# Query tiles, score products and the next batch's probabilities moved in a fused attention and mixer kernel

## The chip, the cores and the metric

One core of a Trainium2 chip runs the whole program. The metric is the time of one execution on the device in microseconds (us); the time of a kernel is the median of its runs.

## What is computed

There are eight batches (B = 8) of 576 tokens with 8 heads of 64 channels and 32 memory slots. Each batch goes through an attention with a small memory, a low-rank token mixer with a two-layer network of width 2048, and a gated network with a spatial product:

```python
a = exp(phi - max(phi, axis=tokens)); a = a / (sum(a, axis=tokens) + 1e-9)
k_m, v_m = a^T k, a^T v                       # per head, 32 x 64
scores = q k_m^T / 8; attn = softmax(scores)  # 576 x 32 per head
x = concat_heads(attn v_m)                    # 576 x 512
u = x + (x^T U V)^T
y = u + relu(u w_ch1) w_ch2                   # 512 -> 2048 -> 512
h = relu(y w_in); u2, v = halves of h
vn = (v - mean) / sqrt(var + 1e-6)
out = (u2 * (w_spatial vn + b_spatial)) w_out
```

## The kernel before

Most products are made in float16 with each operand split into a high and a low part, three products for one. TensorE (PE) is given work nearly without a gap, batch after batch. For batch b the stages are: the first-weight product with relu (in batches 2 to 7 line 954, its results taken out by lines 958 to 966), the second-weight product (line 920 in batches 2 to 7, in a form with seven block products; line 875 in batch 1; line 815 in batch 0), both in two halves of 288 tokens; then the input product of the gate (lines 1107 and 1178), the spatial product (line 1219) and the output product (line 1249).

The attention of the next batch is the generator `att(b + 1)`. It is not a stage of its own: while batch b is worked on, the code of batch b calls `step(nxt)` after every few products, and each call runs `att` up to its next `yield`. So a `yield` more or less, or a call of `step` more or less, moves the attention's instructions against the products of batch b. A scheduler of the framework then sets the order of each engine from this order and the dependences; inside an engine the order is fixed, and an instruction whose input is late holds all that stands behind it.

In `att`, in this order: the maximum over tokens and the exponentials of phi; the products with keys and values (line 578); a transpose (line 598) and its copies `kT` and `vmt32` (lines 604 and 607); the score products `scores(i)` (line 622) for three groups of token tiles, G = (0, 1), (2, 3), (4,), each into two PSUM tiles of the pool `at`, which has three; ScalarE (ACT) copies them to `sT` (line 627); PE transposes `sT` back (line 648); VectorE (DVE) takes the row maximum (652), subtracts it (655), ACT makes the exponential (657), DVE the row sum, its reciprocal and the normalised probability (663 to 667), ACT the high half `ahl[.., 0, :]` (671) and DVE the low half (672). Then PE mixes all five tiles with U (line 681, ten matmuls into one PSUM tile), ACT and DVE make `pst` from it (686, 687), and the generator gives "Z" and then "W". After "W" the mixed probabilities `apr` are made in three pieces (PE lines 538 and 544, maxima on DVE, then 721 and 722) and `att_vmu` (line 740). `step` without `w=True` does not go past "W"; before the change all calls of `step` with `w=True` are in the gate's input product, which the list `V_ORDER` orders.

The query tiles come from DRAM on SyncE's (SP) queue. `load_q(b, s)` takes one of two buffers of the tag "q": tiles 0 and 1 are loaded ahead, and `scores` asks for tile s + 2 when tile s is used, so that the loads of tiles 2 and 3 can only start when the products with tiles 0 and 1 have been made. From batch 3 on, tile 4 has a place of its own in the large buffer `gw`, columns 8064 to 8319, and is loaded in `pre(b)` (line 1472), a batch ahead.

In batch 1 the kernel also prepares, beside its last second-weight product, the block sums of the second weight (`s_prep`, lines 1035 to 1058): four times a load of 1 MB from DRAM (`w2d`), sums and splits on DVE and ACT, and a store. The function `both` calls `step(nxt)` and one step of `s_prep` 32 times in that product.

Of the kernel before, what the change touches and what calls it, by code (L numbers as in the profile page):

```python
# [30 lines left out]
def mixer_kernel(  # L31
# [216 lines left out]
    AT = {}  # L248
# [300 lines left out]
    def att(b):  # L549
# [64 lines left out]
        def scores(i):  # L614
            r = rows(G[i][0])
            n = r * len(G[i])
            ps = [at_tile() for e_ in range(2)]
            for k, s in enumerate(G[i]):
                for p in range(4):
                    for e_ in range(2):  # L620
                        r0 = slice(64 * e_, 64 * e_ + 64)
                        pe.matmul(ps[e_][32 * p:32 * p + 32, k * r:(k + 1) * r], kT[r0, 32 * p:32 * p + 32],
                                  a["q"][s][r0, p, :r], start=True, stop=True)
                load_q(b, s + 2)
            sT[i] = tmp()
            for e_ in range(2):
                act.activation(sT[i][:, e_ * 256:e_ * 256 + n], ps[e_][:, 0:n], func=ACTF.Copy)
# [14 lines left out]
        for gi, grp in enumerate(G):  # L642
# [15 lines left out]
            yield  # L658
            if gi < 2:
                scores(gi + 1)  # L660
            yield
# [9 lines left out]
            act.activation(ahl[:r, s0:s0 + n, 0, :], exs, func=ACTF.Copy)  # L671
            dve.tensor_tensor(out=ahl[:r, s0:s0 + n, 1, :], in0=exs, in1=ahl[:r, s0:s0 + n, 0, :], op=ALU.subtract)
            yield
            yield
        yield
# [3 lines left out]
        for s in range(NST):  # L679
# [3 lines left out]
            if s == 2:  # L683
                yield
        pst = tp.tile([128, 256], F16, tag="pst", name="pst")
        act.activation(pst, pps[:, 0:256], func=ACTF.Copy, scale=2.0 ** -22)
        dve.scalar_tensor_tensor(out=pst[64:96], in0=pps[64:96, 0:256], scalar=2.0 ** -22, in1=pst[64:96],
                                 op0=ALU.mult, op1=ALU.subtract)
        yield
        yield  # L690
# [777 lines left out]
    def pre(b):  # L1468
        if b < B:
            if b > 2:  # L1470
                t = AT[b]["q"][4] = gw[:, 8064:8320].rearrange("p (g c) -> p g c", g=4)
                sp.dma_start(t, qT[b, :, :, 512:S])
            gen[b] = att(b)
            next(gen[b])
# [20 lines left out]
    def step(g, w=False):  # L1495
        if w or not hold.get(id(g)):
            if next(g, None) == "W":
                hold[id(g)] = True
# [74 lines left out]
    for b in range(B):  # L1573
# [3 lines left out]
        elif b == 1:  # L1577
            sq = s_prep()
            w1_phase(b, 0, nofill)

            def both():
                step(nxt)
                next(sq, None)
# [156 lines left out]
```

## Time and profile before

| | |
|---|---|
| median of 3 runs | 1147.14 us (1144.29 to 1148.76) |
| profiled execution | 1148.05 us, span of its records 1146.1 us |
| PE busy, share of the span | 97% |
| DVE, ACT, POOL busy | 74%, 54%, 8% |
| mean granted clock of TensorE | 0.997 |

The span is the time from the first to the last recorded instruction; the profiled execution's own time is 1.95 us longer. Engines work beside each other, so their shares do not add up; with PE at 97%, what matters is each of its gaps and what ended it.

### The profile page before, as it was taken

What the parts mean: (1) busy time and instruction counts of PE and PEld (TensorE: products, weight loads), DVE (VectorE), ACT (ScalarE), POOL (GpSimd) and SP (SyncE); (2) the same over time, 40 slices, a digit from 0 to 9 for tenths busy, and PEclk for the clock granted to TensorE, in tenths of its full rate; (3) what the DMA queues carried; (4) which work ended last, traced back from release to release, by engine and by line L of the source; (5) the groups of instructions that cost most, each with busy time, mean ns of one, the idle gap of its engine ahead of it and who ended that gap; (6) DMA issues with size and microseconds to landing.
All of it is one profiled execution on the core that took longest, in us unless ns stands there. A gap on an engine that the chain in (4) does not pass through costs nothing.

```text
span 1146.1 us, 29691 instructions
## 1 busy us (share of the span) xinstructions
PE 1114.4 (97%) x12365; PEld 867.6 (76%) x12365; DVE 844.5 (74%) x2217; ACT 620.0 (54%) x1350; POOL 89.5 (8%) x316
## 2 busy tenths in 40 slices
PE   8899999999999999999999999999999999999998
PEld 6466667767667896788867887678967888679966
DVE  5767688869786786867776787867868677766854
ACT  4768764736456454564465453564545643653543
POOL 2101011000010001100010000100011000100000
PEclk9999999999999999999999999999999999999999
DMA  9769741340526331442315303253204303130201
GB/s 357 309 258 343 264 170 58 117 146 28 193 76 205 93 112 36 146 150 79 126 59 194 122 22 129 93 203 98 113 35 141 138 20 127 38 116 2 102 27 42
DMA packets 54854, 145.72 MB, mean 127 GB/s; under 512 B 7808, under 2 KB 37248, under 8 KB 43584
## 3 DMA queue, kind: packets, MB, share of 16 engines
q1 hardware_dynamic: 54208, 143.16, 35.4%
q8 instruction: 96, 1.57, 0.6%
q10 hardware_dynamic: 512, 0.67, 0.2%
q14 instruction: 38, 0.31, 0.1%
HBM read 120.32 MB, written 23.49 MB: 125 GB/s over the span
## 4 chain that ended last, share of the span: by engine, by line
PE 74%; DVE 11%; ACT 6%; DMA 5%; issue 2%; POOL 1%; SPq 0%; ACTq 0%; DVEq 0%; POOLq 0%
PE mm L920 17%; PE mm L954 13%; PE mm L1219 10%; PE mm L1249 8%; PE mm L1178 6%; PE mm L1107 5%; PE mm L815 3%; DMA qt<-in_qT_dram 2%; PE at L756 2%; PE at L578 2%; PE mm L792 1%; PE mm L875 1%; DMA q<-in_qT_dram 1%; PE mm L838 1%; DVE yhl L1074 1%
## 5 line engine op out<-in xcount | busy, mean ns | idle before, releaser
L920 PE MATMUL mm<-gw,w2r 128*128 128x144 f16 x2304 | 170.6, 226 | 0.0
L920 PEld LDWEIGHTS <-w2r 128*128 128x128 f16 x2304 | 152.6, 98 | 7.9 <-issue 2.7
L954 PE MATMUL mm<-apr,z 128*128 128x288 f16 x1152 | 155.1, 286 | 0.0
L954 PEld LDWEIGHTS <-z 128*128 128x128 f16 x1152 | 109.7, 98 | 28.3 <-issue 2.0
L958 ACT ACTIVATE wsr<-mm 128x288 f32<-128x288 f32 x192 | 78.3, 408 | 95.2 <-PE mm L954 51.4
L920 PE MATMUL mm<-gw,wa 128*128 128x144 f16 x1728 | 128.8, 226 | 0.0
L1219 PE MATMUL mm<-wsr,gw 128*128 128x288 f16 x896 | 114.3, 286 | 1.7 <-ACT gw L1182 1.6
L920 PEld LDWEIGHTS <-wa 128*128 128x128 f16 x1728 | 111.1, 98 | 4.6 <-issue 2.0
L1219 PEld LDWEIGHTS <-gw 128*128 128x128 f16 x896 | 85.6, 98 | 32.1 <-issue 9.6
L1178 PE MATMUL mm<-yhl,gw 128*128 128x288 f16 x768 | 99.4, 286 | 0.0
L1249 PE MATMUL mm<-ghl,wa 128*128 128x288 f16 x768 | 97.8, 286 | 0.0
L1249 PEld LDWEIGHTS <-wa 128*128 128x128 f16 x768 | 74.4, 98 | 22.8 <-issue 3.8
L1178 PEld LDWEIGHTS <-gw 128*128 128x128 f16 x768 | 73.4, 98 | 18.6 <-issue 0.6
L960 DVE TENSOR_TENSOR wsr<-wsr 128x288 f32<-128x288 f32 x96 | 44.0, 459 | 57.7 <-ACT wsr L958 57.7
L1107 PE MATMUL mm<-gw,yhl 128*128 128x512 f16 x384 | 85.6, 379 | 0.0
L942 DVE TENSOR_TENSOR gw<-wsr,gw 128x720 f16<-128x720 f32 x96 | 85.5, 901 | 0.0
L1234 ACT ACTIVATE ghl<-gw,ysc 128x288 f16<-128x288 f32 x64 | 34.2, 535 | 83.2 <-DVE gw L1233 83.2
L941 ACT ACTIVATE gw<-wsr 128x720 f16<-128x720 f32 x96 | 76.4, 795 | 0.5
L1107 PEld LDWEIGHTS <-yhl 128*128 128x128 f16 x384 | 36.9, 98 | 41.8 <-DVE yhl L1074 0.5
L815 PE MATMUL mm<-gw,w2r 128*128 128x288 f32 x256 | 66.7, 409 | 0.0
L1113 DVE BATCH_NORM_STATS2 tiny<-tmp 128x6 f32<-128x512 f32 (+1 forms) x40 | 25.6, 639 | 46.5 <-ACT tmp L1111 46.4
L815 PEld LDWEIGHTS mm<-gw,w2r 128*128 128x128 f32 x256 | 47.3, 190 | 15.2 <-issue 2.1
(312 smaller groups left out, 1857.3 us busy)
## 6 DMA issues: line engine op xcount, KB each, us to landing
wa<-w1d SPq DMA_DIRECT2D x22, 1024.0 KB, 5.1
kvt<-in_kv_dram SPq DMA_DIRECT2D x28, 516.0 KB, 5.3
gw<-wid SPq DMA_DIRECT2D x12, 1024.0 KB, 7.9
wsr<-wsd SPq DMA_DIRECT2D x7, 1440.0 KB, 6.4
out_dram<-tmp SPq DMA_DIRECT2D x64, 144.0 KB, 1.9
qt<-in_qT_dram SPq DMA_DIRECT2D x28, 256.0 KB, 3.5
gw<-in_w_dram SPq DMA_DIRECT2D x6, 1024.0 KB, 8.3
wa<-wod SPq DMA_DIRECT2D x6, 1024.0 KB, 4.7
```

Of the source, the lines that this page charges most:

```text
L815: pe.matmul(ps, w2r[:, f, d * 128:(d + 1) * 128], AT[0]["g"][:, f, :], start=False, stop=(f == 15))
L920: pe.matmul(ps[:, dd * QH:(dd + 1) * QH], w(c, dd, 1 - x), gs[:, m, c, y, :], start=(first and c == 0 and dd == 0 and i == 0), stop=(end a ...
L941: act.activation(h, X[:, 3:8], func=ACTF.Copy)
L942: dve.tensor_tensor(out=gs[:, 2:7, c, 1, :], in0=X[:, 3:8], in1=h, op=ALU.subtract)
L954: pe.matmul(ps, a["z"][:, k, x, f * 128:(f + 1) * 128], a["apr"][:, k, y, sl], start=(i == 0), stop=(i == 5))
L958: act.activation(o, pair(ps), func=ACTF.Relu, scale=CG)
L960: dve.tensor_tensor(out=X[:, 4:6], in0=X[:, 2:4], in1=X[:, 1:3], op=ALU.subtract)
L1107: pe.matmul(ps, yhl[:, k, x, s * 128:(s + 1) * 128], wih[:, k, 0, 1 - y, :], start=(i == 0), stop=(i == 11))
L1178: pe.matmul(ps, wih[:, k, 1, 1 - x, d * 128:(d + 1) * 128], a["yhl"][:, k, y, sl], start=(i == 0), stop=(i == 11))
L1219: pe.matmul(pss[d], vn[:, s, x if s < 4 else 0, ds], wsh[:, s, th, 1 - y, :], start=(s == 0 and i == 0), stop=(s == 4 and i == 1))
L1234: act.activation(ghl[:, d, 0, sl], u2, func=ACTF.Identity, scale=sgt)
L1249: pe.matmul(ps, (wo0 if b else woh)[:, k, 1 - x, d * 128:(d + 1) * 128], a["ghl"][:, k, y, sl], start=(i == 0), stop=(i == 11))
```

## The change

Five edits. From batch 3 on the third query tile (tile 2) gets a place of its own in `gw`, columns 8320 to 8831, and is loaded in `pre(b)` beside tile 4. When tile 0 is used, tile 3 is asked for; when tile 1 is used, tile 2 (which from batch 3 on is already there). The score products of the later groups are issued after the low and high halves of the first group: from batch 3 on both groups at once, in batches 1 and 2 one group after each group's halves. In the mix with U a second `yield` stands after the third tile, and one `yield` fewer behind `pst`. In batch 1 `both` steps the attention of batch 2 in its calls 1 to 7 and then in every third, from call 9 on with `w=True`.

```diff
@@ -621,7 +621,7 @@
                         r0 = slice(64 * e_, 64 * e_ + 64)
                         pe.matmul(ps[e_][32 * p:32 * p + 32, k * r:(k + 1) * r], kT[r0, 32 * p:32 * p + 32],
                                   a["q"][s][r0, p, :r], start=True, stop=True)
-                load_q(b, s + 2)
+                load_q(b, 3 - s if s < 2 else s + 2)
             sT[i] = tmp()
             for e_ in range(2):
                 act.activation(sT[i][:, e_ * 256:e_ * 256 + n], ps[e_][:, 0:n], func=ACTF.Copy)
@@ -656,8 +656,6 @@
                               in1=mxs[:r, :n * 8].unsqueeze(2).to_broadcast([r, n * 8, M]), op=ALU.subtract)
             act.activation(ex[:r, 0:n * 256], ex[:r, 0:n * 256], func=ACTF.Exp, scale=0.125)
             yield
-            if gi < 2:
-                scores(gi + 1)
             yield
             sm = tiny(16)
             dve.tensor_reduce(out=sm[:r, :n * 8], in_=ex3, axis=AX.X, op=ALU.add)
@@ -670,7 +668,12 @@
             s0 = grp[0]
             act.activation(ahl[:r, s0:s0 + n, 0, :], exs, func=ACTF.Copy)
             dve.tensor_tensor(out=ahl[:r, s0:s0 + n, 1, :], in0=exs, in1=ahl[:r, s0:s0 + n, 0, :], op=ALU.subtract)
+            if gi == 0 and b > 2:
+                scores(1)
+                scores(2)
             yield
+            if gi < 2 and b < 3:
+                scores(gi + 1)
             yield
         yield
         yield
@@ -682,11 +685,11 @@
                           start=(s == 0 and y == 0), stop=(s == NST - 1 and y == 1))
             if s == 2:
                 yield
+                yield
         pst = tp.tile([128, 256], F16, tag="pst", name="pst")
         act.activation(pst, pps[:, 0:256], func=ACTF.Copy, scale=2.0 ** -22)
         dve.scalar_tensor_tensor(out=pst[64:96], in0=pps[64:96, 0:256], scalar=2.0 ** -22, in1=pst[64:96],
                                  op0=ALU.mult, op1=ALU.subtract)
-        yield
         yield
         yield "Z"
 
@@ -1468,8 +1471,9 @@
     def pre(b):
         if b < B:
             if b > 2:
-                t = AT[b]["q"][4] = gw[:, 8064:8320].rearrange("p (g c) -> p g c", g=4)
-                sp.dma_start(t, qT[b, :, :, 512:S])
+                for s, o in ((2, 8320), (4, 8064)):
+                    t = AT[b]["q"][s] = gw[:, o:o + 4 * rows(s)].rearrange("p (g c) -> p g c", g=4)
+                    sp.dma_start(t, qT[b, :, :, s * 128:s * 128 + rows(s)])
             gen[b] = att(b)
             next(gen[b])
 
@@ -1578,8 +1582,12 @@
             sq = s_prep()
             w1_phase(b, 0, nofill)
 
+            nb = [0]
+
             def both():
-                step(nxt)
+                nb[0] += 1
+                if nb[0] < 8 or nb[0] % 3 == 0:
+                    step(nxt, nb[0] > 8)
                 next(sq, None)
 
             y0 = w2_phase(b, 0, lambda: step(nxt), lambda f: fl.until(s2, min(f + 3, 16)))
```

The calls of `att` are numbered by the batch they prepare: `b > 2` in `att` is what runs during batches 2 to 6.

**ACT's queue, first half of the second-weight product of batch 2 (the same in batches 3 to 6).** Names are as in the section on the kernel; 128x256 is a group of two tiles, 128x64 the group of one. Before:

```order
L999 ACTIVATE y_4430<-mm 128x2x144
L604 ACTIVATE t1k<-at 64x128 x2
L627 ACTIVATE tmp<-at 128x256 x2
L637 ACTIVATE vmt<-t1k,sc 128x128
L657 ACTIVATE tmp<-tmp 128x512
L627 ACTIVATE tmp<-at 128x256 x2
L671 ACTIVATE ahl<-tmp 128x2x256
L958 ACTIVATE wsr<-mm 128x288
```

And now:

```order
L1002 ACTIVATE y_4431<-mm 128x2x144
L604 ACTIVATE t1k<-at 64x128 x2
L627 ACTIVATE tmp<-at 128x256 x2
L637 ACTIVATE vmt<-t1k,sc 128x128
L657 ACTIVATE tmp<-tmp 128x512
L627 ACTIVATE tmp<-at 128x256 x2
L627 ACTIVATE tmp<-at 128x64 x2
L669 ACTIVATE ahl<-tmp 128x2x256
```

The copies of the third group (128x64) have come forward from the second half to the place right behind those of the second group. On PE at this place the order was four transposes (line 648), 12 products of line 920, the 16 score products of group 1, and products again; now it is four transposes, 24 products, the 16 score products of group 1, the first 4 of group 2, 4 products, the last 4 of group 2 (which wait for ACT), and products. In the second half the mix (line 681) was 6 matmuls, 6 products, 4 matmuls, 24 products; now it is 6 matmuls, 18 products, 4 matmuls, 12 products.

**SP's queue, from the end of batch 1 to the first half of batch 2.** Before:

```order
L122 DMA wa<-w1d 128x4096 x2
L1472 DMA gw<-in_qT_dram 128x4x64
L1254 DMA out_dram<-tmp 128x288 x3
...
L258 DMA e<-in_phi_dram 128x4x256
L259 DMA e<-in_phi_dram 64x256
L275 DMA kvt<-in_kv_dram 128x1032
L281 DMA qt<-in_qT_dram 128x4x128 x4
L131 DMA wsr<-wsd 128x5760
```

And now:

```order
L122 DMA wa<-w1d 128x4096 x2
L1476 DMA gw<-in_qT_dram 128x4x128
L1476 DMA gw<-in_qT_dram 128x4x64
L1257 DMA out_dram<-tmp 128x288 x3
...
L258 DMA e<-in_phi_dram 128x4x256
L259 DMA e<-in_phi_dram 64x256
L275 DMA kvt<-in_kv_dram 128x1032
L281 DMA qt<-in_qT_dram 128x4x128 x3
```

One of the four query loads in the middle of the first half (tiles 2 and 3 of this attention, tiles 0 and 1 of the next) has moved to the end of the batch before, ahead of three output stores.

**DVE's queue, batch 1, at the last of the four pieces of `s_prep`, now.** L1042 to L1048 are the sums of `s_prep` (lines 1039 to 1045 before), L725 the low halves of `apr`, L744 that of `vmu`.

```order
L1042 TENSOR_TENSOR wa<-wsr 128x512
L161 TENSOR_REDUCE tiny<-mm 128x1
L165 TENSOR_REDUCE tiny<-mm 128x1
L174 RECIPROCAL sc<-sc 128x1
L1044 TENSOR_TENSOR wa<-wa,wsr 128x512
L735 RECIPROCAL rq<-rq 128x1
L736 RECIPROCAL rq<-sc 128x1
L1046 TENSOR_TENSOR wa<-wsr 128x512
L725 SCALAR_TENSOR_TENSOR apr<-at,sc,apr 128x384 x2
L725 SCALAR_TENSOR_TENSOR apr<-at,sc,apr 128x2x192
L744 SCALAR_TENSOR_TENSOR vmu<-t1k,rq,vmu 128x256
L1048 TENSOR_TENSOR wsr<-wsr,wa 128x512
```

Before, the four sums stood here with one maximum between them (L165), and L722 and L741 (now L725 and L744) stood far behind, among the statistics of the gate's input product. On PE the matmuls of lines 538 and 544 have moved from between the products of lines 1107 and 1178 to between those of line 875, behind the 54th, 72nd and 90th of 192.

## Rows read from the trace of the kernel before

**Rows 1.** The page, part 1: busy us of each engine (share of the span) xinstructions
```profile
PE 1114.4 (97%) x12365; PEld 867.6 (76%) x12365; DVE 844.5 (74%) x2217; ACT 620.0 (54%) x1350; POOL 89.5 (8%) x316
```

**Rows 2.** Waits of PE, whole span: us in total, times, longest us
```profile
PE at L622 <- DMA qt<-in_qT_dram: 7.8, 10, 2.1
...
PE at L681 <- ACT ahl L671: 3.7, 5, 0.7
...
PE mm L159 <- DVE dgb L153: 2.9, 2, 2.6
...
PE mm L875 <- DVE w2r L171: 0.5, 1, 0.5
```

**Rows 3.** Timeline of PE, batches 2 to 5: start us, us, what, xcount [idle before]
```profile
390.18 0.61 PE L648 MATMUL at<-ident,tmp 128*128 128x128 f32 x4
...
393.10 1.11 PE L920 MATMUL mm<-gw,wa 128*128 128x144 f16 x15
...
523.25 0.61 PE L648 MATMUL at<-ident,tmp 128*128 128x128 f32 x4
...
523.69 0.91 PE L920 MATMUL mm<-gw,wa 128*128 128x144 f16 x12
...
527.13 0.45 PE L622 MATMUL at<-qt,t1k 64*32 64x128 f32 x16 [1.88 <-DMA qt<-in_qT_dram]
...
527.51 2.05 PE L920 MATMUL mm<-gw,wa 128*128 128x144 f16 x30
...
657.66 0.60 PE L648 MATMUL at<-ident,tmp 128*128 128x128 f32 x4
...
661.56 2.05 PE L920 MATMUL mm<-gw,wa 128*128 128x144 f16 x30
...
791.72 0.60 PE L648 MATMUL at<-ident,tmp 128*128 128x128 f32 x4
...
794.36 2.05 PE L920 MATMUL mm<-gw,wa 128*128 128x144 f16 x30
```

**Rows 4.** Timeline of ACT, batch 5, same place
```profile
794.19 0.63 ACT L657 ACTIVATE tmp<-tmp 128x512 f32<-128x512 f32 x1
...
794.73 0.64 ACT L627 ACTIVATE tmp<-at 128x256 f32<-128x256 f32 x2
```

**Rows 5.** Timeline of PE, batch 3, second half
```profile
567.62 0.28 PE L681 MATMUL at<-ahl,u3h 128*128 128x256 f16 x1 [0.74 <-ACT ahl L671]
...
568.17 1.66 PE L920 MATMUL mm<-gw,w2r 128*128 128x144 f16 x24
```

**Rows 6.** Timeline of PE, SP and DVE, batch 1, second-weight product, first half
```profile
242.19 6.96 SPq L281 DMA_DIRECT2D qt<-in_qT_dram  x4
...
246.60 0.68 PE L622 MATMUL at<-qt,t1k 64*32 64x128 f32 x16 [2.15 <-DMA qt<-in_qT_dram]
...
249.84 0.69 DVE L663 TENSOR_REDUCE tinyw<-tmp 128x16 f32<-128x512 f32 x1 [3.53 <-ACT tmp L657]
```

**Rows 7.** Timeline of PE and DVE, batch 1, second half and what follows
```profile
276.27 23.69 PE L875 MATMUL mm<-gw,w2r 128*128 128x288 f16 x192
...
296.87 0.69 DVE L1039 TENSOR_TENSOR wa<-wsr 128x512 f32<-128x512 f32 x1 [1.35 <-DMA wsr<-w2d]
...
322.43 1.64 DVE L722 SCALAR_TENSOR_TENSOR apr<-at,sc,apr 128x384 f16<-128x384 f32 x3
...
326.42 0.23 PE L159 MATMUL mm<-dgb,onesb 128*128 128x128 bf16 x1 [2.63 <-DVE dgb L153]
```

**Rows 8.** The view of tile qt: ns min/median/max of an issue; landing of all its loads
```profile
L281 SPq DMA_DIRECT2D qt<-in_qT_dram x30: 539/568/1633, 91.3 to 923.3; - x30
...
DMA to landing us min/median/max: 2.5/3.5/8.0
```

**Rows 9.** Timeline of PE, batch 0, second half
```profile
131.08 1.00 PE L622 MATMUL at<-qt,t1k 64*32 64x128 f32 x32 [0.51 <-DMA qt<-in_qT_dram]
```

## The prediction

> **What bounds the kernel now.** First the busy shares: PE is busy for 97% of the span [rows 1], so time can only come out of PE's gaps. Then PE's waits [rows 2]: 7.8 us for query tiles at the score products (line 622), 3.7 us at the mix with U (line 681), five times 0.74, for ACT's high half of the last tile, 2.9 us at line 159 for DVE, of which 2.63 in one place, and 0.5 us for the split weights of batch 1. Then each place in the timeline. In batches 2 to 6 the reader sees the transposes of group 0 (line 648), 12 products of line 920, the score products of group 1, which wait for their tiles, and products again [rows 3]; PE has other products ready, but they stand behind the waiting one in its queue. From the start of the transposes (call it T) to the products behind the scores it takes 2.92, 4.26, 3.90 and 2.64 us in batches 2 to 5, and batch 6 reads as batch 5. In the second half of each batch PE comes to the last tile of the mix before ACT and DVE have it [rows 5]. In batch 1 there are two single stalls: 2.15 us for a query tile, with DVE standing idle 3.53 us behind it [rows 6], because ACT's copy of group 1 stands ahead of group 0's exponential in ACT's queue; and 2.63 us in the gate's input product, where DVE is late [rows 7].
>
> **First halves of batches 2 to 6.** One product of line 920 is 62 ns: 24 in 1.66 us [rows 5] less 12 in 0.91 us [rows 3], over 12. The new order is worked out from T. The transposes end at T + 0.44 (523.25 to 523.69 [rows 3]), 24 products take 1.5, so the score products of group 1 start at T + 1.94. One tile's products and the step back to line 920 take 0.38 (527.13 to 527.51 [rows 3]); two tiles, without waits, are done at about T + 2.4, and the first part of group 2 at T + 2.5. Its second part needs a fourth PSUM tile out of a pool of three, which comes free when ACT has made its first copy of group 1. That copy stands behind the exponential, and here the trace gives its place: the exponential starts at T + 2.47, the next instruction of ACT 0.54 later, and a pair of copies takes 0.64 [rows 4], with T at 791.72 [rows 3]; so the first is done at T + 3.35 and PE can go on at T + 3.4. Four products (0.25) and a step (0.2) fill the time to T + 2.95: a new wait of about 0.45 us. With 0.3 for the last matmuls and the step back, line 920 goes on at T + 3.7 with 28 of its products made. Before, 12 were made by then; with the other 16 (1.0 us) the five places stood at T + 3.92, 5.26, 4.90, 3.64 and 3.64. The differences are +0.22, +1.56, +1.20, -0.06 and -0.06: **2.9 us gained**, and it pays for the products of group 2, which were in the second half. Bounds: without the wait for the PSUM tile 5 times 0.45, 2.2 us more; with an ACT that is one exponential later (0.54) 2.7 us less.
>
> This needs tile 3 in time. It is asked for when tile 0 is used, first of three instead of second of four, and is wanted near T + 2.2. In batch 3 the load that was first in line (then tile 2) was there by 527.13 less the second tile's wait of 1.88, 525.2 or T + 2.0, and the second one at T + 3.9 [rows 3]. So the first place in line is enough, by only some tenths of a us. Tile 2 costs nothing where it is loaded now: its issue on SP is 0.57 us [rows 8] ahead of output stores, SP waits there for the spatial product already, and it has a whole batch to land; if that cover failed it would cost these 0.57 us on SP, not on PE.
>
> **Second halves of batches 2 to 6.** The mix now has 12 more products (0.75 us) ahead of its last four matmuls, and 12 fewer behind them. What ends the mix is the chain of DVE and ACT that began with the first half's maximum; DVE does the same work in it (two y-additions and a maximum come ahead of group 1's probabilities, but all of them stood ahead of the last tile's before too). I take its end as fixed, so PE comes out of the mix at the same time with 12 products fewer to do: **5 times 0.75 = 3.75 us**. The wait that remains is about 0.4 us, since PE has also lost the score products of group 2 here. Bounds: 1.0 us more if the chain ends earlier with ACT freed of two copies, and, if the displaced y-additions delay it by 0.75, nothing gained.
>
> **Batch 1, first half.** 12 more products of line 875 (192 in 23.69 us [rows 7], 0.123 each) stand ahead of group 1's scores: PE comes 1.48 us later to them. But tile 2, which is used first, is now the second load: 0.57 us later [rows 8]. It landed 4.4 us after its issue (242.19 to 246.60 [rows 6]). 2.15 - 1.48 + 0.6 leaves a wait of 1.3 us, 0.85 gained. ACT's exponential is now ahead of the copies, so DVE does not stand idle for 3.53 us and the 0.5 us wait for the split weights [rows 2] goes: **1.3 us**. Bounds 0 and 2.6.
>
> The Trainium skill (DMA: Bandwidth & Descriptors, "Anatomy of one DMA") gives, for DMAs issued from GpSimd, a fixed cost of some 2.0 us plus the bytes over 436 GB/s, an estimate of 2.6 us for the 256 KB of a query tile. By it both tiles would be there before PE, and the sum would be 1.3 us lower. The trace has 2.5 us as the shortest and 3.5 us as the median landing [rows 8], and 4.4 at this place, so the trace's figure is used.
>
> **Batch 1, second half.** The pieces of `apr` leave the gate's input product, where DVE's backlog costs 2.63 us, and join `s_prep` in the second-weight product. PE's matmuls move with them and cost the same. DVE takes 1.64 us for the three low halves [rows 7]; with three maxima over the same columns at a like pace and the small steps I estimate 4.5 us in all. They find little room: the 1.35 us in which DVE waits for a load at 296.87 [rows 7] are eaten by what now stands ahead of it, so that `s_prep` ends up to 3 us later, and the maximum of y with it, whose scale the gate's products need. PE comes later too, by the matmuls that moved, and I put the waits that come back at half of the 3 us: **2.6 - 1.5 = 1.1 us gained**. Bounds: 2.6 gained, if DVE keeps up, and 1 lost, if the reload of the weight is later still: the next phi load now goes ahead of the last of them on SP.
>
> **Batch 0** has one wait of 0.51 us for a query tile [rows 9], and 9 more products ahead of it; but its last mixing comes later against a DVE that is full. I take **0.3 us**, bounds -1.5 and 0.5.
>
> **The sum**: 2.9 + 3.75 + 1.3 + 1.1 + 0.3 = 9.3 us. The profiled execution took 1148.05 us, so 1138.7; the median of the runs lies 0.9 lower, which gives **1138 us**.
>
> **Rivals.**
> *Given back (chance 0.22).* The query waits go, but the wait for the PSUM tile is 1.0 instead of 0.45 us (-2.7) and batch 1 gives nothing (-2.4): 9.3 - 5.1 = 4.2 us, about 1143. For it speaks that batches 5 and 6 show almost no query wait to remove, so the new wait counts there in full; against it, that ACT's place at T + 3.0 is steady [rows 4]. The Trainium skill (Perfetto Trace Analysis, "Optimization Strategy") reads a gap that repeats as a possible sign of too few buffers for the next tile; four PSUM tiles out of three is such a case, and no row of before shows its price.
> *All waits go (0.17).* The products fill the wait for the PSUM tile, the mix does not wait, batch 1 loses both stalls: 2.9 + 2.2 + 3.75 + 1.0 + 2.6 + 2.6 + 0.5 = 15.6 us, 1132. For it speaks that every such wait has ready products behind it; against it, that DVE's chains do not get shorter.
> *Slower (0.05).* Tile 3 lands late in every batch. Its products hold the queue, then ACT's copy, then group 2, one behind the other, so each us goes into the path in full. From a landing 3.5 us after its issue [rows 8] there is 0.3 us in hand; the gain is gone when five batches lose 9.3 / 5 = 1.9 us each, at a landing of 5.7 us, and at 7 us the time is 1154. The rows have 8.0 us as the longest [rows 8], so it can be; against it, the slow one in batch 3 was the second in line [rows 3], and tile 3 is now first.
>
> **How the numbers follow.** The forecast has 0.56, with its own range of 1135 to 1141.4. A measurement of this kernel tells a change of some 0.5% (5.7 us) from none. The forecast and the second rival lie beyond that, less a part of the forecast near its upper end: faster 0.71. The first rival and that part: same 0.24. Slower 0.05. The range leaves out the slower rival and the lower end of the second: 1132 to 1145.
>
> **What would show it.** The waits at line 622 for query tiles gone from batches 2 to 6 and replaced by one of ACT of about 0.45 us; the wait at line 681 down from 0.74 to about 0.3 to 0.4 with DVE's last half at the same distance from the first half's maximum; 1 to 1.5 us at line 622 in batch 1; the stall of 2.63 us at line 159 gone and shorter ones a few us earlier. The prediction is wrong if ACT reaches the copies later than T + 3.0, if DVE's chain grows by the y-additions, or if `s_prep` gets longer than by 3 us.

## The result

The changed kernel takes 1135.66 us (median of 6 runs, 1134.62 to 1136.32), the kernel before 1147.01 us (6 runs): a ratio of 0.9905, 95% interval 0.989 to 0.992. The forecast was 1138, its own range 1135 to 1141.4. The profiled execution took 1134.62 us with a span of 1132.8 us, 13.4 us less than the profiled one of before. PE is busy for 98% of the span.

The page, part 1, after (busy us of each engine, share of the span, instructions):

```profile
PE 1112.1 (98%) x12362; PEld 868.4 (77%) x12365; DVE 842.9 (74%) x2217; ACT 619.6 (55%) x1350; POOL 89.5 (8%) x316
```

The waits of PE, after (us in total, times, longest):

```profile
PE mm L1110 <- ACT yhl L1076: 1.3, 1, 1.3
PE at L684 <- DVE ahl L670: 1.2, 6, 0.2
...
PE at L622 <- ACT tmp L627: 1.1, 5, 0.2
...
PE at L622 <- DMA qt<-in_qT_dram: 0.7, 1, 0.7
...
PE mm L159 <- DVE dgb L153: 0.2, 1, 0.2
```

Against [rows 2]: the 7.8 us for query tiles are 0.7, in batch 1 alone; the wait at the mix went from 3.7 us on ScalarE and 0.8 on VectorE to 1.2 on VectorE (line 684 is 681 of before); the 2.9 us at line 159 are 0.2. Two waits are new: five times 0.21 us at the score products for ScalarE's copy, which frees the fourth PSUM tile, and 1.3 us at line 1110 in batch 1.

The timeline of PE, batch 3, first half, after; to be read against [rows 3]:

```profile
516.86 0.61 PE L648 MATMUL at<-ident,tmp 128*128 128x128 f32 x4
517.30 1.66 PE L923 MATMUL mm<-gw,wa 128*128 128x144 f16 x24
518.89 0.45 PE L622 MATMUL at<-gw,t1k 64*32 64x128 f32 x16
519.13 0.42 PE L622 MATMUL at<-qt,t1k 64*32 64x128 f32 x16
519.39 0.32 PE L622 MATMUL at<-gw,t1k 64*32 64x64 f32 x8
519.64 0.42 PE L923 MATMUL mm<-gw,wa 128*128 128x144 f16 x4
520.28 0.32 PE L622 MATMUL at<-gw,t1k 64*32 64x64 f32 x8 [0.21 <-ACT tmp L627]
520.53 1.05 PE L923 MATMUL mm<-gw,wa 128*128 128x144 f16 x14
```

The timeline of ACT at the same place, to be read against [rows 4]:

```profile
519.32 0.63 ACT L657 ACTIVATE tmp<-tmp 128x512 f32<-128x512 f32 x1
519.86 1.02 ACT L627 ACTIVATE tmp<-at 128x256 f32<-128x256 f32 x4
```

From the transposes (T = 516.86) PE now makes 24 products without a gap, all three score products without a wait for a tile, and four products; then it stands 0.21 us and is back at line 923 at T + 3.67. ACT's exponential starts at T + 2.46 and the first copy at T + 3.00. Before, that point was at T + 4.26 with 12 products made instead of 28.

The timeline of PE, batch 3, second half, after; to be read against [rows 5]:

```profile
557.10 0.71 PE L684 MATMUL at<-ahl,u3h 128*128 128x256 f16 x5
558.03 0.27 PE L684 MATMUL at<-ahl,u3h 128*128 128x256 f16 x1 [0.22 <-DVE ahl L670]
558.13 1.29 PE L923 MATMUL mm<-gw,w2r 128*128 128x144 f16 x18
559.26 0.76 PE L684 MATMUL at<-ahl,u3h 128*128 128x256 f16 x4
559.86 0.91 PE L923 MATMUL mm<-gw,w2r 128*128 128x144 f16 x12
```

The wait for the last tile's high half is gone from the list; 0.22 us for group 1's low half stands ahead of the first part of the mix, and 12 products are left behind the second.

The timeline of PE, batch 1, after; to be read against [rows 6, 7]:

```profile
245.63 0.67 PE L622 MATMUL at<-qt,t1k 64*32 64x128 f32 x32 [0.71 <-DMA qt<-in_qT_dram]
...
308.61 5.47 PE L1110 MATMUL mm<-gw,yhl 128*128 128x512 f16 x24 [1.34 <-ACT yhl L1076]
```

The timeline of DVE, batch 1, second half, after; to be read against [rows 7]:

```profile
295.49 0.16 DVE L735 RECIPROCAL rq<-rq 128x1 f32<-128x1 f32 x1 [1.03 <-POOL rq L147]
...
302.34 0.24 DVE L153 TENSOR_SCALAR dgb<-identb,tiny 128x128 bf16<-128x128 bf16 x1
```

The query wait is 0.71 us, the 2.63 us at line 159 are gone, and 1.34 us came back at line 1110: VectorE stands 1.03 us for GpSimd in the middle of the fourth block sum, and the maximum of y, whose scale line 1110 needs, comes after it. The chain that ended last at this place begins earlier, at the landing of the fourth block (292.48), and runs through GpSimd's steps and VectorE's queue; run 8 asks which part of it counts.

**Where the time came from.** I read the starts of stages off PE's timeline, since in batches 2 to 6 one execution repeats them to some hundredths of a us: a batch from its first product of line 957 (954 before), its "first half" up to the first such product of the second half, its "second half" from there to the next batch. The sums over batches 2 to 6, and batch 1 from its first product of line 841 (838), in us, for the profiled execution of each kernel (the experiments below tell of the others):

| kernel | batch 1 | five first halves | five second halves |
|---|---|---|---|
| before | 142.03 | 202.64 | 464.06 |
| place and load order alone | 141.92 | 196.50 | 464.10 |
| changed | 138.16 | 199.62 | 458.80 |
| changed, without the place | 138.37 | 202.94 | 458.71 |
| changed, mix as before | 138.15 | 199.65 | 462.73 |
| changed, batch 1's steps as before | 141.18 | 200.43 | 458.94 |
| changed, scores of batches 0 and 1 early | 140.94 | 199.65 | 458.60 |
| changed, group 2 a group later | 138.85 | 195.71 | 465.05 |
| changed, group 2 a step later | 138.49 | 195.71 | 460.51 |
| changed, mix a step later | 138.16 | 199.61 | 456.72 |
| changed, batch 1's steps denser | 138.33 | 199.64 | 458.58 |
| group 2 and mix a step later | 138.57 | 195.70 | 458.42 |
| group 2 a step, mix two steps later, a step more in batch 1 | 139.86 | 195.71 | 456.97 |
| group 2 a step, mix two steps later | 139.30 | 195.81 | 456.97 |

Batch 1 is less steady. Runs 4 and 5 (group 2 a step and a group later) have the changed kernel's code there and took 138.49 and 138.85 us against 138.16. And in batch 1 the granted clock of TensorE fell to half (1.2 instead of 2.4 GHz) for some us in three of these executions: of the kernel before, of run 2 (the place alone) and of run 7 (batch 1's steps as before). In the kernel before it came with the end of the query stall of 2.15 us [rows 6]. Stretches of 2 us there; the third number from the end is PE's granted clock:

```profile
246.00:248.00 2.00, 1.40 (x26) 0.59 (x34) 0.31 (x1) 0.00 (x0) 0.00 (x0) 0.61 0.03 9
248.00:250.00 2.00, 2.00 (x24) 1.04 (x14) 0.16 (x1) 1.36 (x4) 0.00 (x0) 0.53 0.34 76
```

From 246.60 to 251.07 PE took 4.47 us for 32 score matmuls and 18 products of line 875. The 32 take 0.61 in the changed kernel, 18 products at 0.123 take 2.2, and two more steps between them 0.2 to 0.4 (the prediction took 0.2 for one); so I estimate that some 1.3 of batch 1's 3.87 us are the clock's, in this execution. Whole times go with it too: of the nine executions of the kernel before beside run 12 the fastest, 1144.53 us, had a mean granted clock of 1.000, the slowest, 1152.08 us, 0.993.

The change gave 3.02 us in the first halves, 5.26 in the second, 3.87 in batch 1, together 12.15 of the 13.3 us between the spans. The other 1.1 lie ahead of batch 1. They are not the change's to claim: up to batch 0's first product of line 795 the fourteen kernels, with the same code there, took from 37.3 to 39.5 us, one 40.5, and the rest of batch 0 took 175.6 us in the changed kernel and 177.1 in one whose code is the same there.

### The profile page after: what moved, and what is told of

It is laid out like the page before. It is cut to its first block, busy times and chain, and to the rows that moved or that the text cites. A ratio compares the mean times of both kernels' runs of the same rounds, so it can differ in the third digit from the quotient of the medians.

```text
span 1132.8 us, 29695 instructions
## 1 busy us (share of the span) xinstructions
PE 1112.1 (98%) x12362; PEld 868.4 (77%) x12365; DVE 842.9 (74%) x2217; ACT 619.6 (55%) x1350; POOL 89.5 (8%) x316
## 4 chain that ended last, share of the span: by engine, by line
PE 77%; DVE 12%; ACT 5%; DMA 2%; issue 2%; POOL 1%; SPq 0%; ACTq 0%; DVEq 0%; POOLq 0%
PE mm L923 17%; PE mm L957 13%; PE mm L1222 10%; PE mm L1252 8%; PE mm L1181 6%; PE mm L1110 6%; PE mm L818 4%; PE at L759 2%; PE at L578 2%; PE mm L795 1%; PE mm L841 1%; DMA gw<-in_kv_dram 1%; PE mm L878 1%; DMA wsr<-w2d 1%; DVE tmp L655 1%
```

## The experiments

Each diff is against the changed kernel unless it says otherwise; unchanged parts are left out. Ratios are to the kernel before, timed beside it on the same chip, with 95% intervals.

**1. Without the place.**

```diff
-                for s, o in ((2, 8320), (4, 8064)):
+                for s, o in ((4, 8064),):
...
-                load_q(b, 3 - s if s < 2 else s + 2)
+                load_q(b, s + 2)
```

> The changed kernel, but tile 2 is loaded as in the kernel before (no place of its own, first of four loads, tile 3 second). Everything else as changed. Theory: the place is needed, because the second load in line is late where the first is not. Tile 3 was there at T + 2.5, 3.9, 3.5 and at most T + 2.3 in batches 2 to 5 of the kernel before; it is wanted at T + 2.2 now, and where it is late it puts ACT's copy and the fourth PSUM tile behind it. Expected: a wait for a query tile at the score products of 0.3, 1.7, 1.3, 0 and 0 us in batches 2 to 6, about 2 to 3 us of the gain lost, so some 8.5 to 9.5 us faster than before. Rival: the later position alone is enough, nothing lost (11.4 us faster than before, no wait for a query tile).

Measured: 1137.9 us (1137.63 to 1139.61), ratio 0.9915 (0.9889 to 0.9941). The waits of PE without the place:

```profile
PE at L622 <- DMA qt<-in_qT_dram: 3.6, 6, 1.3
```

Its timeline of PE, batch 3, first half:

```profile
517.89 0.61 PE L648 MATMUL at<-ident,tmp 128*128 128x128 f32 x4
...
521.58 0.45 PE L622 MATMUL at<-qt,t1k 64*32 64x128 f32 x16 [1.20 <-DMA qt<-in_qT_dram]
```

The five first halves lost 0.75, 1.24, 1.31, 0.01 and 0.01 us: 3.3 in all, at the places that the theory named. A position that is later by 12 products does not replace the place: tile 3, second in line, still arrives at T + 3.7 in batch 3 (521.58 against 517.89).

**2. The place alone**, on the kernel before.

```diff
-                t = AT[b]["q"][4] = gw[:, 8064:8320].rearrange("p (g c) -> p g c", g=4)
-                sp.dma_start(t, qT[b, :, :, 512:S])
+                for s, o in ((2, 8320), (4, 8064)):
+                    t = AT[b]["q"][s] = gw[:, o:o + 4 * rows(s)].rearrange("p (g c) -> p g c", g=4)
+                    sp.dma_start(t, qT[b, :, :, s * 128:s * 128 + rows(s)])
...
-                load_q(b, s + 2)
+                load_q(b, 3 - s if s < 2 else s + 2)
```

> The kernel before with two of the five edits alone: tile 2's own place and load, and tile 3 asked for first. Score products, mix and the function of batch 1 as before. Theory: tile 2 waits no more, but at the old position PE comes to tile 3 some 0.9 us earlier than in the changed kernel, about T + 1.4, and tile 3 lands near T + 2.0: a wait of about 0.6 us stays in batches 2 to 4, none in 5 and 6, where almost none was. From T to line 920 again about 2.6 to 3.3 us against 2.9, 4.3, 3.9, 2.6, 2.6: 2 to 2.5 us gained in these places, and with batch 1 about 0 (its tile 2 is now second in line, 0.6 us later): 1.5 to 2.5 us faster than before. Rival: the transfer is limited by bandwidth and not by its place in the queue, tile 3 is as late as it was: nothing gained.

Measured: 1141.33 us (1139.19 to 1142.73), ratio 0.9926 (0.9905 to 0.9947). The timeline of PE with the place alone, first halves of batches 3 and 5:

```profile
520.11 0.61 PE L648 MATMUL at<-ident,tmp 128*128 128x128 f32 x4
...
521.89 0.45 PE L622 MATMUL at<-qt,t1k 64*32 64x128 f32 x16
...
785.77 0.45 PE L622 MATMUL at<-gw,t1k 64*32 64x128 f32 x16
786.02 0.42 PE L622 MATMUL at<-qt,t1k 64*32 64x128 f32 x16
```

Theory and rival fell, on the high side. The first halves gained 0.52, 2.10, 2.01, 0.75 and 0.76 us, 6.14 in all. I had tile 3 at T + 2.0; it is used at T + 1.78 in batch 3. What I had read off [rows 3] was only an upper bound: 525.2, from the wait of the second load. A row of the kernel before that I had passed over, from the same timeline of PE, shows the first load in line used at T + 1.55:

```profile
524.80 0.45 PE L622 MATMUL at<-qt,t1k 64*32 64x128 f32 x16 [0.19 <-DMA qt<-in_qT_dram]
```

Batches 5 and 6 showed 0.45 and 0.33 us of listed wait (batch 5 at 793.29 and 793.97) and gained 0.75 and 0.76: with their tiles there, the two groups of score products stand back to back (785.77 and 786.02), where a tile that was just awaited cost PE more than the wait that the view lists.

**3. The mix as before.**

```diff
             if s == 2:
                 yield
-                yield
...
+        yield
         yield
         yield "Z"
```

> The changed kernel with the yields of the mix with U as before (one after the third tile, two behind pst), so that 6 instead of 18 products stand inside the mix and 24 instead of 12 behind it. Theory: the chain of DVE and ACT ends the mix at a fixed time, so the 12 products (0.75 us) are lost in each of five batches, 3.75 us: some 7.6 us faster than before, with the wait at the last tile of the mix 0.22 + 0.75, about 0.95 us. Rival 1: the 0.32 us by which the chain has become shorter also came from this edit, 5.3 us lost, 6 us faster than before. Rival 2: the chain waits for products through the additions of y and moves with them, nothing lost.

Measured: 1138.31 us (1137.6 to 1138.7), ratio 0.9915 (0.989 to 0.994). Each second half lost 0.78 us (3.93 in all), the 12 products of the theory. The waits of PE:

```profile
PE at L684 <- ACT ahl L669: 2.3, 5, 0.7
...
PE at L684 <- DVE ahl L670: 1.9, 10, 0.2
```

That is 0.84 us a batch, (2.3 + 1.9) / 5, against 0.95 expected. VectorE's queue decides between theory and rival 1. From the y-addition of the second half (line 994 or 997) to the last low half (672 or 670), batch 3, in us: 13.03 before (554.57 to 567.60), 12.70 changed, 12.70 here, 12.71 with the mix a step later. The chain is fixed against PE's mix, and its 0.33 us have another cause.

**4. Group 2 a step later, and 5. a group later.**

```diff
                 scores(1)
-                scores(2)
             yield
-            if gi < 2 and b < 3:
-                scores(gi + 1)
+            if gi < 2 and b < 3 or gi == 0:
+                scores(gi + (1 if b < 3 else 2))
             yield
```

and for the second

```diff
                 scores(1)
-                scores(2)
             yield
-            if gi < 2 and b < 3:
+            if gi < 2 and (b < 3 or gi == 1):
                 scores(gi + 1)
```

> As the run with group 2 one group later, but only one step later: its score products stand alone at the end of the first half. VectorE's queue is that of the other run, with y's maximum behind group 1's low half. Theory: the first halves gain 0.2 us each at equal products (the wait gone, one step of PE fewer), the second halves lose the 0.32 us of the chain: even with the changed kernel, 0 to 1 us slower, 10.4 to 11.4 us faster than before. Rival: the chain's length does not depend on the place of y's maximum, and it is 1 us faster than the changed kernel.

> The changed kernel, but from batch 3's attention on group 2's score products come one group later, behind group 1's halves in the second half of the product; group 1's stay where they are. No fourth PSUM tile is asked for in the first half. Theory: two things come apart. The first halves gain the wait of 0.21 us and the two steps of PE around group 2, 0.64 us each at equal products; and the second halves lose the 0.32 us by which VectorE's chain had become shorter, because y's maximum falls back behind group 1's low half in its queue as in the kernel before. In sum 0.3 us per batch, 1.6 us faster than the changed kernel, 13 us faster than before. Rival: with group 2's products, copies and transposes in the second half PE itself is late at the mix (0.5 us of work against 0.22 of wait), and it is even or up to 1 us slower than the changed kernel (10.4 to 11.4 us faster than before).

Measured: a step later 1133.45 us (1131.41 to 1137.46), ratio 0.9877 (0.9846 to 0.9907); a group later 1138.16 us (1136.84 to 1138.94), ratio 0.9905 (0.9884 to 0.9926). Both gain 0.78 us in each first half, where the step-later kernel goes from the 24 products and group 1 straight on. In the second halves the one loses 0.34 and the other 1.25 us. The timeline of DVE, batch 3, second half, in the kernel before:

```profile
554.57 0.46 DVE L994 TENSOR_TENSOR y<-mm,y 128x288 f32<-128x288 f32 x1 [0.82 <-PE mm L931]
...
564.95 0.69 DVE L672 TENSOR_TENSOR ahl<-tmp,ahl 128x512 f16<-128x512 f32 x1
565.56 0.74 DVE L165 TENSOR_REDUCE tiny<-y 128x1 f32<-128x576 f32 x1
...
567.60 0.42 DVE L672 TENSOR_TENSOR ahl<-tmp,ahl 64x256 f16<-64x256 f32 x1 [0.17 <-ACT ahl L671]
```

The same in the changed kernel:

```profile
546.58 0.46 DVE L997 TENSOR_TENSOR y<-mm,y 128x288 f32<-128x288 f32 x1 [0.82 <-PE mm L934]
...
556.31 0.74 DVE L165 TENSOR_REDUCE tiny<-y 128x1 f32<-128x576 f32 x1
...
557.30 0.68 DVE L670 TENSOR_TENSOR ahl<-tmp,ahl 128x512 f16<-128x512 f32 x1
...
559.28 0.42 DVE L670 TENSOR_TENSOR ahl<-tmp,ahl 64x256 f16<-64x256 f32 x1 [0.18 <-ACT ahl L669]
```

And with group 2 a step later:

```profile
554.72 0.69 DVE L670 TENSOR_TENSOR ahl<-tmp,ahl 128x512 f16<-128x512 f32 x1
555.33 0.75 DVE L165 TENSOR_REDUCE tiny<-y 128x1 f32<-128x576 f32 x1
...
557.36 0.42 DVE L670 TENSOR_TENSOR ahl<-tmp,ahl 64x256 f16<-64x256 f32 x1 [0.17 <-ACT ahl L669]
```

With group 2 moved, y's maximum (line 165) falls back behind group 1's low half, where it stood before, and the chain is 13.02 us in both runs (544.34 to 557.36; 547.87 to 560.89). So the 0.33 us hang on the order of VectorE's queue, whose work is the same in both: in the changed kernel an addition of y (line 1014) stands ahead of group 1's product (line 665) and the maximum ahead of its low half, in the others they stand behind. From start to start 0.11 us of the difference lie at the product, which in the others follows its reciprocal directly, and 0.14 at the low half, which there waits for ScalarE's half. That ScalarE was freed of two copies is not the cause: its exponentials start at the same distance from the chain's start, 6.62 and 8.78 us before, 6.62 and 8.77 now. The first run is 2.2 us better than the changed kernel by its stages, not even: I had counted 0.45 us for group 2's products at their new place, and there, ahead of a mix that waits for the chain, they cost nothing (the second halves lost the chain's 0.33 us and no more). The second is 2.3 us worse by its stages; it met a wait that neither theory named. The waits of PE with group 2 a group later:

```profile
PE at L648 <- DVE tmp L655: 5.0, 5, 1.0
```

Its timeline of PE, batch 3, second half:

```profile
554.60 0.27 PE L648 MATMUL at<-ident,tmp 128*64 128x128 f32 x1 [0.99 <-DVE tmp L655]
```

Group 2's two score tiles and the transposed tile of group 1 fill the pool of three, so group 2's transposes wait until VectorE has read group 1's: four tiles out of three again, at 0.99 us instead of 0.21.

**6. The mix a step later.**

```diff
         yield
+        yield
         pps = at_tile()
...
-        yield
         yield "Z"
```

> The changed kernel with the whole mix with U one step (6 products) later, and one yield fewer behind pst. Theory: VectorE's and ScalarE's chain ends at a fixed time, PE still waits 0.22 us for group 1's low half and up to 0.2 us inside the last four matmuls, and 6 more products (0.37 us) ahead of the mix take up both: 0.2 to 0.4 us in each of five batches, 1.0 to 2.0 us faster than the changed kernel, 12.4 to 13.4 us faster than before, with no wait at the mix left. Rival: what follows the mix (pst, the pieces of apr) is late by as much, and a wait comes up in the gate's input product: even.

Measured: 1133.08 us (1131.04 to 1135.19), ratio 0.9862 (0.9836 to 0.9888). Each second half gained 0.36 us (the last one 0.62, of which some 0.25 is the changed kernel's own: runs 1 and 7 to 9 have that half 0.25 shorter too). No row of line 685, the mix, is left among PE's waits. The theory holds.

**7. Batch 1's steps as before, and 8. denser steps.**

```diff
-                nb[0] += 1
-                if nb[0] < 8 or nb[0] % 3 == 0:
-                    step(nxt, nb[0] > 8)
+                step(nxt)
```

and for the second

```diff
-                if nb[0] < 8 or nb[0] % 3 == 0:
+                if nb[0] < 8 or nb[0] % 2 == 0:
```

> The changed kernel with the function of batch 1 that steps the attention as before (one step per call, never past the W mark), so that the pieces of apr go back into the gate's input product. Theory: the stall of some 2.6 us at line 159 comes back and the 1.3 us at line 1110 goes, 1.0 us lost: 10.4 us faster than before. Rival 1: the gain of the edit is nothing (11.4 us faster). Rival 2: the edit gained the whole 2.6 us and the stall at line 1110 has another cause, which stays: 8.8 us faster.

> The changed kernel, but in batch 1's last product the attention is stepped in every second call instead of every third after call 7, so that the pieces of apr end some 3 us earlier and stand ahead of the fourth block sum in VectorE's queue instead of inside it. Theory: the 1.34 us at line 1110 come from VectorE standing 1.03 us for GpSimd at line 735 in the middle of the fourth block sum; ahead of it that wait falls into the time in which the load of the fourth block is awaited anyway (0.70 us). The maximum of y comes 1.0 to 1.5 us earlier and 1.0 to 1.3 us of the stall go: 12.4 us faster than before. Rival: the load or the backlog of the splits decides, the order of the pieces does not matter: 11.4 us faster than before.

Measured: steps as before 1138.07 us (1135.98 to 1140.56), ratio 0.9912 (0.9884 to 0.994); denser 1136.01 us (1133.94 to 1138.79), ratio 0.9889 (0.9864 to 0.9914). Without the edit batch 1 is 3.02 us longer, not 1.0. The timeline of PE in batch 1, without the edit:

```profile
322.28 0.23 PE L159 MATMUL mm<-dgb,onesb 128*128 128x128 bf16 x1 [2.63 <-DVE dgb L153]
322.34 2.62 PE L1181 MATMUL mm<-yhl,gw 128*128 128x288 f16 x12
324.90 1.47 PE L759 MATMUL at<-wa,vmt 64*32 64x512 f16 x24
```

Stretches of 2 us there, with PE's granted clock:

```profile
322.00:324.00 2.00, 1.72 (x10) 1.20 (x11) 1.73 (x12) 1.87 (x8) 0.00 (x0) 0.70 0.02 4
324.00:326.00 2.00, 2.00 (x29) 0.61 (x26) 1.39 (x4) 1.97 (x4) 1.57 (x4) 0.50 0.00 0
```

The stretch with the end of the same stall in the kernel before [rows 7]:

```profile
326.00:328.00 2.00, 1.58 (x13) 1.15 (x13) 1.73 (x14) 1.94 (x7) 0.00 (x0) 1.00 0.00 0
```

The stall of 2.63 us is the same, but here the clock fell behind it, to half of full speed: the 12 products of line 1181 and the 24 of line 759 took 3.96 us (322.34 to 326.30), where before they took 2.33 (326.49 to 328.82). That is 1.6 us on top. Another 0.4 lies in the first half (58.24 against 57.87 us), with a longer query wait (1.21 against 0.71), so about 1.0 us is the edit's own, as the theory had it. In run 2, whose code is the old one here, the clock fell behind this stall too (0.53 and 0.61 in the stretches 322 to 324 and 324 to 326). What makes it fall in the one execution and not in the other is open. The denser steps moved the wait and did not remove it: 0.65 us at line 159 (290.36) and 0.97 at 1110 (310.01) in place of 1.34, and batch 1 took 138.33 us against 138.16. The order of the pieces in VectorE's queue is not what decides; the rival holds. The load counts: the wait at line 159 goes with the time that the fourth block takes to land, 0.2 us after 5.2 in the changed kernel, 0.48 after 5.5 in run 10, 0.69 after 5.9 in run 5, 0.80 after 6.1 in run 9.

**9. The score products of batches 0 and 1 early.**

```diff
             yield
+            if gi < 2 and b < 3:
+                scores(gi + 1)
             yield
             sm = tiny(16)
...
             yield
-            if gi < 2 and b < 3:
-                scores(gi + 1)
             yield
```

> The changed kernel with the score products of batches 1 and 2's attentions (those that run in batches 0 and 1) back between the exponential and the row sum. The load order (tile 3 before tile 2) stays. Theory: the first half of batch 1's last product gets back its stall for a query tile (2.15 us, and 0.57 more because tile 2 is now second in line), the step between the two tiles and the wait for the split weights: 3 to 3.6 us there and up to 0.5 us in batch 0, some 7.5 to 8 us faster than before. Rival, the sizes of the prediction: 1.3 and 0.3 us lost, 9.8 us faster than before.

Measured: 1138.58 us (1136.46 to 1140.12), ratio 0.9917 (0.9889 to 0.9945). Batch 1 lost 2.8 us, batch 0 nothing (175.61 against 175.58 us). PE's timeline, batch 1, in this run:

```profile
247.57 0.67 PE L622 MATMUL at<-qt,t1k 64*32 64x128 f32 x32 [1.43 <-DMA qt<-in_qT_dram]
...
252.18 0.35 PE L622 MATMUL at<-qt,t1k 64*32 64x64 f32 x16 [1.19 <-DMA qt<-in_qT_dram]
...
260.89 0.28 PE L841 MATMUL mm<-apr,z 128*128 128x288 f16 x1 [0.56 <-ACT tmp L845]
```

Three waits, 3.2 us in sum, against 0.9 in the changed kernel, make the first half 2.1 us longer (59.93 against 57.87). The other 0.7 go with the wait at line 159 behind the late fourth block (run 8), which run 5 has with the changed kernel's code. The rival's 1.3 us was the prediction's sum with the load order in it, which stays here; its terms for the position alone, 1.48 and 0.5, make 2.0, as measured.

**10 to 12. Towards a better version.** Run 10 is runs 4 and 6 in one. Run 11 has the mix two steps later and, in batch 1, one step more between scores(0) and its transposes; against run 4:

```diff
         scores(0)
         yield
+        if b == 2:
+            yield
...
         yield
+        yield
+        yield
         pps = at_tile()
...
-        yield
         yield "Z"
...
-                if nb[0] < 8 or nb[0] % 3 == 0:
+                if nb[0] < 9 or nb[0] % 3 == 0:
```

Run 12 is run 11 without the first and the last of these edits, those of batch 1.

> Two of the earlier runs in one: group 2's score products one step later (0.44 us gained in each of five batches by its markers) and the mix one step later (0.36 us). Theory: they add up where the second one had no wait left, and do so more here, since the chain ends 0.32 us later and PE's wait at the mix is 0.2 us longer: 0.8 us in each batch, 4.0 us faster than the changed kernel, 15.3 us faster than before. Rival: the mix ends so late that the pieces of apr or the gate's input product wait for it: 2.2 us faster than the changed kernel.

> As the run before, with the mix two steps later instead of one, and in batch 1 one step more between group 0's score products and its transposes (6 products, 0.74 us) with the calls of the function of batch 1 shifted by one. Theory: the second step takes up the rest of PE's wait at the mix (about 0.17 us inside the last four matmuls), 0.1 to 0.2 us in each of five batches; in batch 1 the wait for a query tile, 0.5 to 1.4 us in the runs so far, goes down by 0.74: 1 to 1.5 us faster than the run before, 16.5 us faster than before. Rival: no wait is left at the mix and batch 1's attention is later as a whole, with DVE behind in the second half: the same as the run before or up to 1 us slower.

> The changed kernel with group 2's score products one step later and the mix two steps later; batch 1 as changed, without the step that the last run added there. Theory: the second step of the mix brings 0.34 us in each of five batches beside the run with one step, as the last run's markers show, and batch 1 is back at its time in the changed kernel, 1.3 us less than in the last run: 1.7 us faster than the run with one step, 17 us faster than before. Rival: the mix that ends two steps later makes the pieces of apr in batch 1 late, as the last run had it: 15.5 us faster than before.

Measured: 1131.55 us (1131.0 to 1132.63), ratio 0.9843 (0.9824 to 0.9861); 1130.11 us (1128.64 to 1131.41), ratio 0.983 (0.981 to 0.985); 1131.24 us (1130.25 to 1131.57), ratio 0.9846 (0.9823 to 0.987). Run 10 adds up as expected: 3.9 us in the five first halves and 0.4 in the second. The second step of the mix brought 1.5 us more there (runs 11 and 12), but in run 12 0.7 went in batch 1, where the mix is later too (a wait of 0.86 us at line 159, though the fourth block landed after 5.1 us). The added step of run 11 took batch 1's query wait down to 0.18 us and put 1.74 us at line 159. The intervals of the three overlap; all three beat both kernels, and which is best stays open.

## Why the prediction was right, and where it was not

**First halves of batches 2 to 6: 2.9 forecast, 3.02 measured.** Line 923 resumed at T + 3.67 with 28 products, as worked out (T + 3.7); the fourth PSUM tile came free at T + 3.42. PE stood 0.39 us between its four products (519.64 and 0.25) and 520.28, near the 0.45 forecast; the view lists 0.21 of it. Each of the five places came within 0.05 us of its forecast. The experiments show what the sum hid: it is the difference of two larger terms. The place gives 6.1 us. The later position takes 3.1 of them back in the first halves and, without the mix's edit, returns 1.4 in the second (464.10 to 462.73): on top of the place it costs 1.8 us in batches 2 to 6. Run 4 shows that group 2 alone is what costs there: with group 1 later and group 2 moved on the first halves take 195.71 us, 0.8 less than with the place alone.

**Second halves: 3.75 forecast, 5.26 measured.** The mechanism held: 12 products, 0.78 us each time, against a chain that does not care where the mix stands. "I take its end as fixed" was the mis-sized step: the chain ended 0.33 us earlier, by the order of VectorE's queue (run 5). I had named the bound (1.0 us more), for another reason, ScalarE's freed copies, which the traces rule out.

**Batch 1, first half: 1.3 forecast, 3.0 measured, in part by the clock.** The stretch up to the second half's first second-weight product went from 60.86 to 57.87 us. Run 2, with the old position, already has 59.27, though its listed waits are 0.2 us longer than in the kernel before: its clock stayed at 1.00 in this half, where the profiled execution of the kernel before lost some 1.3 us (an estimate, above) that I had not counted. Besides, two products had stood there between tile 2's and tile 3's score products, with PE's steps to and fro. The position itself gives 1.4 against run 2 and 2.1 against run 9. The wait came down to 0.71, not 1.3, because the tile landed 3.7 us after its issue instead of the 4.4 I took; in run 4, with the same code here, it took 4.4 and the wait was 1.41. The wait for the split weights went from 0.46 to 0.21, not to nothing.

**Batch 1, second half: 1.1 forecast, 0.9 measured.** 2.63 us went, 1.34 came back at line 1110 and 0.2 at line 159, for the named reason, a backlog of VectorE ahead of y's scale. That the 1.5 us put down for them were met is in part luck: from the first product of the second half to the last split of `s_prep` (line 171) it took 26.9 us before and 30.8 now, 3.9 more, past the 3 that the prediction had named as a sign of being wrong.

**Batch 0: 0.3 forecast**, not to be told from the spread ahead of batch 1.

**Rivals.** *Given back*: the wait for the PSUM tile is there and smaller. The Trainium skill (Perfetto Trace Analysis, "Optimization Strategy") reads such a repeating gap as a possible sign of too few buffers, and the trace agrees: 5 times 0.21 us here, 5 times 0.99 in run 5. *All waits go* did not come: 0.71 and 1.34 us are left in batch 1 and the small waits elsewhere; the time lies 2.3 us under the forecast, of which the second halves make 1.5; the rest cannot be split, with the clock in it. *Slower* did not come: tile 3 was used without a wait in all five batches. It can be late all the same: in run 7 one of the five had a query wait of 0.8 us. The Trainium skill's cost of a DMA (DMA: Bandwidth & Descriptors, "Anatomy of one DMA"), given for DMAs issued from GpSimd, makes 2.6 us as an estimate for a tile and would have left no wait in batch 1; 0.2 to 1.4 us were measured there, so the trace's own landing time was the better figure. (By it the time would be 1.3 us lower and the sum of the gains higher, not lower as the prediction has it.)

## What to carry to other kernels

A transfer that waits for a buffer is best given the buffer: the place alone made 6.1 us, and a later position that asked for a fourth PSUM tile out of three lost part of it again. Where PE stands in line for a chain of other engines, put ready products ahead of the waiting instruction until no wait is left; here each step was worth what it covered. And read a sum that came out right by its parts: one run for each edit showed a loss inside a gain. Look at the granted clock of both executions before a difference of a stage is put down to an edit.

## What was not expected

After the same stall of 2.63 us the granted clock fell to 0.50 in the execution of run 7, and fell in that of run 2, and stayed at 1.00 in that of the kernel before, a difference of 1.6 us between run 7 and before; in the kernel before it had fallen behind the shorter stall of 2.15 us. And a tile that PE had to wait for cost more than the listed wait: 0.45 us listed and 0.75 gained in batch 5, 0.33 and 0.76 in batch 6.
